# A re-planned adaLN transformer block: second-norm scalings with a GpSimd alternative, a 6/2 split of the modulation weight load, and a new order plan

## The chip, the cores and the metric

The kernel runs on one core of a Trainium2 chip. A core has TensorE (PE in the profile, with its weight loads shown as PEld), VectorE (DVE), ScalarE (ACT), GpSimd (POOL), and SyncE (SP), which here only issues transfers. The metric is the device time of one execution in microseconds.

## The reference

One transformer block on 2048 tokens of width 1024. Six modulation vectors come from a small conditioning vector; attention has 32 query heads of width 32 and one shared key and value head; the feed-forward part has a hidden width of 3584.

```
mod = silu(c) @ w_mod                      # 6 vectors of 1024: sa, ca, ga, sb, cb, gb
h = layernorm(x) * (1 + ca) + sa
q, k, v = h @ wq, h @ wk, h @ wv           # 32 heads of 32 for q, one head of 32 for k and v
x = x + ga * (softmax(q k^T / sqrt(32)) v @ wo)
h = layernorm(x) * (1 + cb) + sb
x = x + gb * ((silu(h @ w1) * (h @ w3)) @ w2)
```

## The kernel before, in words

**Blocks and stages.** The tokens are cut into 8 blocks of 256 (`n`), the heads into 8 groups of four (`f`), the keys into 8 pairs of 128 (`j`). One score step is eight matmuls (`s_exp`): four heads side by side on 32 rows each, two key tiles. There are 8 x 8 x 8 = 512 of them, and each is followed by two ACT exponentials of 128x1024 (tile U<-S). DVE adds pairs of the exponentials (tag `pair`, tile PS<-U) and sums those (tag `av`, PS<-PS), so that PE needs few matmuls for the softmax sums (PB<-PS,ONES); PE also multiplies with V (PB<-U,V). After the eighth head group of a block, `wo` projects, adds to x, and takes the second norm; `slab` (14 per block) does the gate and up products with tanh on ACT and two DVE multiplications; `quarter` (4 per block) does the product with w2. The feed-forward part of block n is laid beside the attention of block n+1, and that of the last block stands alone at the end.

**Second norm.** `wo(n)` makes the normalised rows in XN. For blocks 1 to 6, SP transposes them by two DMA transposes into tile QT (through `h2t`), and then eight VectorE instructions, one per 128 channels, multiply by 1+cb and add sb in place (QT<-QT,MODC, 128x256 bf16; 48 in all). The gate and up matmuls of a block read these eight pieces two at a time and in order. Blocks 0 and 7 go through TensorE transposes and are scaled while being read from PSUM.

**Start of the program.** SP issues the loads in one fixed list: x rows, parts of w_mod, parts of wq. `wm_dma(fld, h)` loads one modulation field in two parts of its eight 128-row chunks, cut by `WSPL`; field 1 is the scale ca, field 0 the shift sa. `mod_cols(fld)` is one group of matmuls per part. The scale goes into the key, value and first query weights (`scale0`), the shift into the biases of k and q (`k_bias`), which the first score needs. The list is: x 0-1, x 2-3, field 1 part 0, x 4-5, field 1 part 1, x 6-7, wq first part, x 8-11, field 0 part 0, field 0 part 1, wq second part, x 12-15.

**What sets the order.** Nothing is ordered by hand after that. The program first records all operations as a graph (`Graph.op`: engine, estimated duration, what is read and written, a due value `vt`, and `alts`, other engines that could do it). `Placer` then walks through a model of the time and decides at build time in which order, and for operations with `alts` on which engine, each is issued. Among operations that could start within a slack of the earliest, it takes the one with the least due value; score matmuls have the least of all. The estimated costs are the durations given to `op`, a price for PE when it changes between score matmuls (mode S), the attention products (mode A) and full matmuls (mode F) (`SWITCH`), and latencies between engines. For POOL it lengthens an operation that starts while a `pair` or `av` addition is on DVE. The steering numbers are in `PLAN`: one entry for each 16 score steps, with two slacks for starts, two rules for changes of mode, and additions to the due values by tag and engine (for example `"slab/pe": -12`). The result is one fixed instruction list per engine; on the chip, each engine works through its own list in order and waits on semaphores.

In `Placer.choose`, an entry is read like this:

```
late, pes, sl, one, hold, off = self.plan[min((self.step + self.SPAN - 1) // self.SPAN, len(self.plan) - 1)]
slack = pes if e == "pe" else sl
```

In profile rows nearly all instructions have line 22, since a helper there plays the recorded calls, so groups are told by tile names.

Of the kernel before, what the change touches and what calls it, by code (L numbers as in the profile page):

```python
# [6 lines left out]
ALU = mybir.AluOpType  # L7
# [35 lines left out]
class Graph:  # L43
# [63 lines left out]
    def alias(self, new, old):  # L107
# [5 lines left out]


PLAN = [
    (0.0, 0.12, 0.2, 1, 0.7,
     {"wo/pe": -19, "mc/pe": 25, "slab/dve": -28, "ln/dve": -40, "k/pe": 5, "mod/pe": 114, "mc/dve": 1}),
    (0.0, 0.12, 0.1, 1, 1.3, {"mc/pe": 27, "q/dve": -2, "ln/pe": 6, "ln/act": 32, "v/pe": 15, "mod/pe": 18}),
    (0.0, 0.12, 0.1, 1, 0.9,
     {"mc/pe": 27, "slab/act": -5, "q/dve": -2, "ln/pe": 6, "ln/act": 32, "v/pe": 15, "mod/pe": 18}),  # L120
    (0.0, 0.12, 0.1, 1, 0.9,
     {"q/pe": -119, "mc/pe": 27, "slab/act": -5, "q/dve": -2, "ln/pe": 6, "ln/act": 32, "v/pe": 15, "mod/pe": 18,
      "kb/pe": -44, "mc/dve": -51}),
    (0.0, 0.16, 0.2, 1, 2.6,
     {"slab/pe": -74, "q/pe": 2, "av/dve": 20, "slab/dve": 32, "slab/act": -7, "q/dve": -2, "mc/dve": 6}),
    (0.0, 0.16, 0.2, 1, 1.6,
     {"slab/pe": -74, "q/pe": 2, "av/dve": 20, "slab/dve": 32, "slab/act": -7, "q/dve": -2, "mc/dve": 6}),
    (0.0, 0.16, 0.2, 1, 1.3,
     {"slab/pe": -74, "q/pe": 2, "av/dve": 20, "slab/dve": 32, "slab/act": -7, "q/dve": -2, "mc/dve": 6}),
    (0.0, 0.13, 0.2, 1, 1.3,  # L130
     {"slab/pe": -74, "q/pe": 2, "av/dve": 20, "slab/dve": 32, "slab/act": -7, "wo/dve": 106, "q/dve": -2,
      "mc/dve": 6}),
    (0.0, 0.13, 0.2, 1, 1.3,
     {"slab/pe": -74, "q/pe": 2, "pair/dve": 22, "av/dve": 20, "slab/dve": 49, "slab/act": -7, "wo/dve": 106,
      "q/dve": -2, "mc/dve": 6}),
    (0.0, 0.11, 0.0, 1, 2.4, {"wo/pe": 4, "slab/pe": 107, "quarter/pe": -2, "q/pe": -26, "an/dve": 4, "q/dve": -119}),
    (0.0, 0.11, 0.02, 1, 2.6,
     {"wo/pe": 4, "slab/pe": 107, "quarter/pe": -2, "q/pe": -26, "an/dve": 4, "q/dve": -119}),
    (0.0, 0.11, 0.02, 1, 2.6,
     {"wo/pe": 4, "slab/pe": 107, "quarter/pe": -2, "q/pe": -26, "an/dve": 4, "q/dve": -119}),  # L140
    (0.0, 0.11, 0.2, 1, 2.6,
     {"wo/pe": 135, "quarter/pe": 20, "mc/pe": -8, "pair/dve": 119, "av/dve": -14, "an/dve": 72,
      "quarter/dve": -26, "wo/dve": 65, "q/dve": -66}),
    (0.0, 0.11, 0.2, 1, 1.4, {"wo/pe": -20, "slab/pe": 107, "q/pe": -26, "an/dve": 54, "q/dve": -119}),
    (0.0, 0.11, 0.02, 1, 3.1,
     {"wo/pe": -20, "q/pe": -26, "mc/pe": -3, "av/dve": 8, "an/dve": 54, "slab/dve": 29, "q/dve": -119}),
    (0.0, 0.11, 0.05, 0, 2.3,
     {"av/pe": -15, "q/pe": -9, "mc/pe": 109, "pair/dve": -1, "an/dve": 4, "slab/act": 15, "q/dve": 7,
      "mc/dve": 6}),
    (0.0, 0.11, 0.2, 1, 2.4,  # L150
     {"wo/pe": 17, "quarter/pe": -15, "mc/pe": -8, "pair/dve": -39, "av/dve": 1, "an/dve": 72,
      "quarter/dve": -26, "wo/dve": 65, "q/dve": -72}),
    (0.0, 0.12, 0.2, 1, 1.3, {"slab/pe": -12, "av/dve": 57}),
    (0.0, 0.11, 0.2, 1, 2.9,
     {"av/pe": -12, "wo/pe": -19, "slab/pe": -9, "quarter/pe": -39, "pair/dve": -2, "an/dve": -117,
      "quarter/dve": -16, "q/dve": -105}),
    (0.0, 0.11, 0.2, 1, 1.9,
     {"av/pe": -12, "wo/pe": -19, "slab/pe": -9, "quarter/pe": -39, "pair/dve": -2, "an/dve": -117,
      "quarter/dve": -16, "q/dve": -105}),
    (0.0, 0.11, 0.2, 1, 1.9,  # L160
     {"av/pe": -12, "wo/pe": -19, "slab/pe": -9, "quarter/pe": -39, "pair/dve": -2, "an/dve": -117,
      "quarter/dve": -16, "q/dve": -105}),
    (0.0, 0.11, 0.2, 0, 0.7,
     {"av/pe": -12, "wo/pe": -19, "slab/pe": -9, "quarter/pe": -39, "pair/dve": -2, "an/dve": -143,
      "quarter/dve": -16, "q/dve": -105}),
    (0.0, 0.11, 0.05, 1, 3.1,
     {"wo/pe": -17, "mc/pe": -8, "av/dve": 1, "an/dve": 47, "slab/act": 11, "quarter/dve": -26, "wo/dve": 86}),
    (0.0, 0.11, 0.05, 1, 3.1,
     {"wo/pe": -17, "mc/pe": -8, "av/dve": 1, "an/dve": 47, "slab/act": 11, "quarter/dve": -26, "wo/dve": 86}),
    (0.0, 0.11, 0.05, 1, 3.1,  # L170
     {"wo/pe": -17, "mc/pe": -8, "av/dve": 1, "an/dve": 47, "slab/act": 11, "quarter/dve": -26, "wo/dve": 86}),
    (0.0, 0.14, 0.2, 0, 0.1, {"slab/pe": -12, "pair/dve": -20, "av/dve": -18, "slab/dve": -24}),
    (0.0, 0.11, 0.05, 0, 3.3,
     {"wo/pe": -17, "mc/pe": -8, "pair/dve": 43, "av/dve": 14, "slab/act": 9, "quarter/dve": -26}),
    (0.0, 0.11, 0.05, 0, 3.3,
     {"wo/pe": -17, "mc/pe": -8, "pair/dve": 43, "av/dve": 14, "slab/act": 9, "quarter/dve": -26}),
    (0.0, 0.11, 0.2, 1, 1.4,
     {"av/pe": -15, "quarter/pe": -3, "q/pe": -9, "mc/pe": 33, "pair/dve": -16, "av/dve": -5, "an/dve": 18,
      "quarter/dve": -37, "q/dve": 7, "mc/dve": 6}),
    (0.0, 0.11, 0.2, 1, 1.4,  # L180
     {"quarter/pe": -3, "q/pe": -9, "mc/pe": 33, "av/dve": -5, "an/dve": 18, "quarter/dve": 74, "q/dve": 7,
      "mc/dve": 6}),
    (0.0, 0.11, 0.0, 1, 1.4,
     {"quarter/pe": -3, "q/pe": -9, "mc/pe": 33, "av/dve": -5, "an/dve": 18, "quarter/dve": 74, "q/dve": 7,
      "mc/dve": 6}),
    (0.0, 0.11, 0.05, 0, 4.1,
     {"wo/pe": -17, "slab/pe": -70, "mc/pe": -8, "pair/dve": 43, "av/dve": 14, "slab/dve": 97, "slab/act": 9,
      "quarter/dve": -26}),
    (0.0, 0.11, 0.2, 0, 3.3,
     {"slab/pe": -13, "quarter/pe": 27, "mc/pe": 61, "slab/dve": -16, "quarter/dve": 6, "wo/dve": 2}),  # L190
]


# [257 lines left out]
def build(nc, x_in, wq_in, wk_in, wv_in, wo_in, w1_in, w3_in, w2_in, c_in, wmod_in, out, S, D, F):  # L451
    G = Graph(nc)
    op = G.op
    NC = D // P
# [43 lines left out]
    MODC = sb("MODC", [P, 4, NC], F32)  # L498
# [87 lines left out]
        dma("sp", dst, x2[tt0 * P:(tt0 + cnt) * P, :].rearrange("(t p) d -> p t d", p=P), ("XL", tt0),  # L586
            cnt * P * D * 2, writes=keys, vt=vt, bw=FAST)

    WSPL = (0, 4, NC)

    def wm_dma(fld, h, vt):
        c0, c1 = WSPL[h:h + 2]
        dma("sp", WM0[:, c0:c1, fld * D:(fld + 1) * D], pc(wmod_in)[:, c0:c1, fld * D:(fld + 1) * D],
            ("WM0", fld, h), (c1 - c0) << 18, writes=[("WM0", fld, h)], vt=vt, bw=FAST)

    def wq_dma(f0, f1, key, vt):
# [18 lines left out]
       writes=["C1"], vt=-1990)  # L615
    op("dve", lambda: [lambda e: e.tensor_scalar(SCC[:, 2, :], SCC[:, 1, :], 0.5, 0.5, ALU.mult, ALU.add)], 0.17,
       reads=["C1"], writes=["C2"], vt=-1990)
    op("dve", lambda: [lambda e: e.tensor_tensor(SCC[:, 3, :], SCC[:, 2, :], SCC[:, 0, :], ALU.mult)], 0.17,
       reads=["C0", "C2"], writes=["C3"], vt=-1990)
    op("dve", lambda: [lambda e: e.tensor_copy(WKR[:, 0], WKV[:, 0].unsqueeze(2).broadcast_to([P, NC, 4, 32]))], 0.45,  # L620
       reads=[("WKV", 0)], writes=["WKR0"], vt=-1600)
# [297 lines left out]
    def h2t(n):  # L919
        return H20 if n == 0 else QT[:, n - 1, :, :]  # L920

    def h2k(n):
        return [("H20", cc) for cc in range(NC)] if n == 0 else [("QT", n - 1, cc) for cc in range(NC)]

    def xk(n, t, qs=range(4)):
        return [("X", n % NX, t, q) for q in qs]

    def wo(n, vt):
        G.tag = "wo"
        for t in range(2):  # L930
            for h in range(2):
                s = Sess()
                for q in range(4):
# [3 lines left out]
                       reads=[(k, *i) for f in range(2 * q, 2 * q + 2) for k, i in (("QT", (n, f)), ("WOG", (f,)))],  # L937
                       writes=[("wo", n, t, h)], vt=vt, mode="F", sess=s, post=0.145)
                xs = X1[:, n % NX, t, h * 512:(h + 1) * 512]
                k = xk(n, t, (2 * h, 2 * h + 1))  # L940
                op("dve", lambda b, xs=xs: [lambda e: e.tensor_tensor(xs, xs, BANK[b], ALU.add)], 0.605,
                   reads=[("wo", n, t, h)] + k, writes=k, vt=vt, sess=s)
            ln_stats(X1[:, n % NX, t, :], 2 * n + t, xk(n, t), vt)
            ln_norm(X1[:, n % NX, t, :], 2 * n + t, xk(n, t), t, vt)
        if 0 < n < NB - 1:
            for t in range(2):
                o = op("sp", lambda t=t: [lambda e: e.dma_start_transpose(h2t(n)[:, :, t * P:(t + 1) * P], XN[t])], 1.2,
                       reads=[("XN", t)], writes=[("h2r", n, t)] + h2k(n), vt=vt - 100, waw=(t == 0), dma=("HT2", t),
                       nbytes=1 << 18)
                o.bw = 200e3  # L950
            for cc in range(NC):
                op("dve", lambda cc=cc: [lambda e: e.tensor_scalar(
                    h2t(n)[:, cc, :], h2t(n)[:, cc, :], MODC[:, 3, cc:cc + 1], MODC[:, 2, cc:cc + 1], ALU.mult, ALU.add)],
                   0.17, reads=[("h2r", n, 0), ("h2r", n, 1), ("MODC", 3, cc // 4), ("MODC", 2, cc // 4)],
                   writes=[h2k(n)[cc]], vt=vt)
            return
        for hh in range(2):
            s = Sess()
# [3 lines left out]
               writes=[("h2", n, hh)], vt=vt, mode="F", sess=s, post=0.145)  # L962
            for k in range(4):
                cc = 4 * hh + k
# [3 lines left out]
                   reads=[("h2", n, hh), ("MODC", 3, hh), ("MODC", 2, hh)], writes=[h2k(n)[cc]], vt=vt, sess=s)  # L968
# [136 lines left out]
    for cc in range(NC):  # L1105
        op("dve", lambda cc=cc: [lambda e: e.tensor_scalar(WQ[:, cc, :], WQ[:, cc, :], MODC[:, 1, cc:cc + 1], None,
                                                           ALU.mult)], 0.43,
           reads=["WQ0", "WQ1", ("MODC", 1)] + [("QBI", f) for f in range(NC)], writes=["WQ0", "WQ1"], vt=-1100,
# [16 lines left out]
    for f in range(NC):  # L1125
        op("dve", lambda f=f: [lambda e: e.tensor_tensor(WO[:, f, :], WO[:, f, :], GAR[:], ALU.mult)], 0.605,
           reads=[("WO", f // 4), ("XN", 0)], writes=[("WOG", f)], vt=20)
# [77 lines left out]
```

## Time and profile before

| what | value |
|---|---|
| median of 3 runs | 1142.18 us (1142.15 to 1142.33) |
| profiled execution | 1142.53 us |
| its span, first to last instruction | 1140.7 us |
| PE, ACT, DVE, POOL busy | 1115.7, 1024.3, 953.9, 38.3 us |
| granted TensorE clock | 1.000 |
| first exponential starts | 30.97 us |
| span 41 to 200 us: PE, ACT busy of 159 | 151.81, 158.37 us |
| span 200 to 1045 us: PE, ACT busy of 845 | 836.15, 829.14 us |
| span 1045 to 1141 us: PE, ACT busy of 96 | 92.76, 8.37 us |

A row of the groups gives busy time, the mean length of one instruction in ns, and the idle time of the engine just before it with what ended that idle time. Lengths of neighbours overlap in the pipeline, so busy time divided by the count is what one of them takes from its engine.

### The profile page before, as it was taken

Reading aid. Unit: us, or ns where it says so; the run is one execution under the profiler, and the core shown is the slowest. Engines: PE = TensorE matmul, PEld = TensorE weight load, DVE = VectorE, ACT = ScalarE, POOL = GpSimd, SP = SyncE. Lnnn points to the kernel's source line nnn. Section 1 sums busy time; section 2 is a strip of 40 time slices with the busy share of each in tenths; the row PEclk is TensorE's granted clock in tenths of the full one; section 3 lists DMA queues with packets and bytes.
Section 4 is the critical chain, followed back from the end, with each engine's and each line's share of the span. In section 5 each row is a group of like instructions: output and inputs, shape, how many; then the busy total and the mean of one; then the engine's idle time right before and its main releaser. Section 6 shows DMA issues by size and latency. Waiting matters only on the chain.

```text
span 1140.7 us, 34695 instructions
## 1 busy us (share of the span) xinstructions
PE 1115.7 (98%) x15538; PEld 756.8 (66%) x15568; DVE 953.9 (84%) x1557; ACT 1024.3 (90%) x1161; POOL 38.3 (3%) x83
## 2 busy tenths in 40 slices
PE   8999999999999999999999999999999999999998
PEld 7644556666577756776567656776577656776887
DVE  7888899998888888888979799888978988888442
ACT  5999999999999999999999999999999999996110
POOL 4100000000000000000000010000100000000000
PEclk9999999999999999999999999999999999999999
DMA  9500379665596668665696659675686658667793
GB/s 345 179 2 1 113 222 245 181 187 155 132 264 194 172 163 221 191 196 154 145 253 196 173 143 236 192 204 131 156 249 192 174 140 231 194 188 202 222 291 118
DMA packets 374291, 209.45 MB, mean 184 GB/s; under 512 B 17536, under 2 KB 365952, under 8 KB 374144
## 3 DMA queue, kind: packets, MB, share of 16 engines
q1 hardware_dynamic: 373712, 207.11, 65.2%
q8 instruction: 122, 2.00, 0.8%
q14 instruction: 25, 0.20, 0.1%
q10 hardware_dynamic: 432, 0.13, 0.0%
HBM read 199.89 MB, written 4.19 MB: 179 GB/s over the span
## 4 chain that ended last, share of the span: by engine, by line
ACT 48%; PE 41%; DVE 8%; DMA 2%; issue 1%; SPq 0%; POOL 0%; DVEq 0%
ACT U L22 44%; PE PB L22 29%; PE S L22 12%; DVE PS L22 4%; ACT HT L22 4%; DVE QT L22 1%; DMA W<-in_A_wq_dram 1%; DVE HT L22 1%; DVE RB L22 1%; DVE X L22 0%; DMA QT<-XNB 0%; SPq L22 0%; DVE ST L22 0%; DVE XNB L22 0%; DVE RC L22 0%
## 5 line engine op out<-in xcount | busy, mean ns | idle before, releaser
L22 ACT ACTIVATE U<-S 128x1024 bf16<-128x1024 f32 x1024 | 962.8, 1105 | 15.7 <-PE S L22 7.7
L22 DVE TENSOR_TENSOR PS<-U 128x2048 bf16<-128x2048 bf16 x256 | 309.1, 1213 | 21.3 <-ACT U L22 19.2
L22 DVE TENSOR_TENSOR PS<-PS 128x1024 bf16<-128x1024 bf16 x368 | 248.9, 685 | 4.0
L22 PE MATMUL PB<-QT,W 128*128 128x256 bf16 x1856 | 230.6, 273 | 0.9 <-DVE RB L22 0.4
L22 PE MATMUL S<-QT,KT 32*128 32x256 bf16 x4096 | 203.4, 273 | 7.8 <-ACT U L22 5.5
L22 PEld LDWEIGHTS PB<-QT,W 128*128 128x128 bf16 x1856 | 169.9, 98 | 49.3 <-issue 26.8
L22 PE MATMUL PB<-W2S,HT 128*128 128x256 bf16 x1512 | 189.8, 273 | 0.0
L22 PEld LDWEIGHTS PB<-W2S,HT 128*128 128x128 bf16 x1512 | 136.9, 98 | 43.8 <-issue 27.2
L22 PEld LDWEIGHTS S<-QT,KT 32*128 32x128 bf16 x4096 | 60.7, 92 | 134.8 <-ACT U L22 122.4
L22 PE MATMUL PB<-U,V 128*32 128x256 bf16 x4032 | 125.6, 273 | 1.6 <-DVE HT L22 1.0
L22 PE MATMUL PB<-QT,HT 128*128 128x256 bf16 x960 | 120.6, 273 | 0.6 <-DVE HT L22 0.3
L22 PEld LDWEIGHTS PB<-U,V 128*32 128x32 bf16 x4032 | 99.7, 96 | 23.4 <-issue 10.8
L22 ACT ACTIVATE HT<-PB 128x512 bf16<-128x512 f32 (+1 forms) x110 | 76.4, 696 | 32.7 <-PE PB L22 32.6
L22 PEld LDWEIGHTS PB<-QT,HT 128*128 128x128 bf16 x960 | 87.7, 98 | 25.8 <-issue 14.0
L22 PE MATMUL PB<-HT,W 128*128 128x256 bf16 (+1 forms) x561 | 98.5, 316 | 2.4 <-issue 1.6
L22 DVE SCALAR_TENSOR_TENSOR HT<-HT,PB 128x512 bf16<-128x512 bf16 x102 | 69.4, 681 | 31.8 <-ACT HT L22 30.9
L22 DVE TENSOR_TENSOR HT<-HT,PB 128x512 bf16<-128x512 bf16 x102 | 69.5, 682 | 15.0 <-PE PB L22 13.2
L22 PEld LDWEIGHTS PB<-HT,W 128*128 128x128 bf16 x576 | 50.2, 97 | 37.0 <-issue 13.9
L22 PE MATMUL PB<-WO,QT 128*128 128x512 bf16 x217 | 54.0, 380 | 1.8 <-issue 1.3
L22 DVE STREAM_TRANSPOSE RB<-PB 128x256 f32<-128x256 f32 x63 | 28.2, 447 | 29.6 <-PE PB L22 29.4
L22 POOL TENSOR_SCALAR RS<-MV 128x1 f32<-128x1 f32 x32 | 11.3, 354 | 1015.4 <-DVE MV L22 1010.4
L22 DVE COPY RB<-PB 128x256 f32<-128x256 f32 x63 | 26.4, 419 | 18.5 <-PE PB L22 18.5
(112 smaller groups left out, 648.9 us busy)
## 6 DMA issues: line engine op xcount, KB each, us to landing
W<-in_B_w_dram SPq DMA_DIRECT2D x150, 512.0 KB, 4.9
W2S<-in_B_w_dram SPq DMA_DIRECT2D x28, 1792.0 KB, 8.3
HT<-in_B_w_dram SPq DMA_DIRECT2D x74, 512.0 KB, 4.9
W2S<-in_w_mod_dram SPq DMA_DIRECT2D x8, 1024.0 KB, 6.8
X<-in_A_x_dram SPq DMA_DIRECT2D x8, 512.0 KB, 6.3
U<-in_w_mod_dram SPq DMA_DIRECT2D x4, 1024.0 KB, 11.4
out_dram<-X SPq DMA_DIRECT2D x7, 512.0 KB, 7.9
U<-in_B_w_dram SPq DMA_DIRECT2D x1, 3584.0 KB, 14.0
```

What stands on the lines that cost most here:

```text
L22: return getattr(e, call[0])(*call[1], **call[2])
```

## The change

Three things change.

The eight scalings per block are given an estimated cost of 0.258 in place of 0.17, and an alternative: the same instruction on POOL at an estimated 0.8. The planner chooses for each. The line `POOLH = True` switches the alternative on.

The cut of the modulation loads moves from 4+4 chunks to 6+2, for both fields (1.5 MB and 0.5 MB in place of 1 MB and 1 MB).

All entries of `PLAN` are replaced (the rest of the new list is left out below). The chooser and its rules stay the same.

```diff
 PLAN = [
-    (0.0, 0.12, 0.2, 1, 0.7,
-     {"wo/pe": -19, "mc/pe": 25, "slab/dve": -28, "ln/dve": -40, "k/pe": 5, "mod/pe": 114, "mc/dve": 1}),
-    (0.0, 0.12, 0.1, 1, 1.3, {"mc/pe": 27, "q/dve": -2, "ln/pe": 6, "ln/act": 32, "v/pe": 15, "mod/pe": 18}),
...
+    (0.0, 0.2, 0.2, 0, 1.3, {"mc/pe": -16, "pair/dve": -90, "av/dve": -32, "k/pe": -82, "k/dve": 48, "mod/pe": 53}),
+    (0.0, 0.16, 0.2, 1, 1.3, {"mc/pe": 77, "pair/dve": -90, "q/dve": -23, "k/pe": -82, "k/dve": 48, "mod/pe": 53}),
...
-    WSPL = (0, 4, NC)
+    WSPL = (0, 6, NC)
...
+    POOLH = True
...
             for cc in range(NC):
                 op("dve", lambda cc=cc: [lambda e: e.tensor_scalar(
                     h2t(n)[:, cc, :], h2t(n)[:, cc, :], MODC[:, 3, cc:cc + 1], MODC[:, 2, cc:cc + 1], ALU.mult, ALU.add)],
-                   0.17, reads=[("h2r", n, 0), ("h2r", n, 1), ("MODC", 3, cc // 4), ("MODC", 2, cc // 4)],
-                   writes=[h2k(n)[cc]], vt=vt)
+                   0.258, reads=[("h2r", n, 0), ("h2r", n, 1), ("MODC", 3, cc // 4), ("MODC", 2, cc // 4)],
+                   writes=[h2k(n)[cc]], vt=vt, alts=[("pool", lambda cc=cc: [lambda e: e.tensor_scalar(
+                       h2t(n)[:, cc, :], h2t(n)[:, cc, :], MODC[:, 3, cc:cc + 1], MODC[:, 2, cc:cc + 1], ALU.mult,
+                       ALU.add)], 0.8)] if POOLH else [])
             return
```

More of the change, by code (lines that the diff above doesn't have):

```diff
@@ L115 @@
 PLAN = [
-    (0.0, 0.12, 0.2, 1, 0.7,
-     {"wo/pe": -19, "mc/pe": 25, "slab/dve": -28, "ln/dve": -40, "k/pe": 5, "mod/pe": 114, "mc/dve": 1}),
-    (0.0, 0.12, 0.1, 1, 1.3, {"mc/pe": 27, "q/dve": -2, "ln/pe": 6, "ln/act": 32, "v/pe": 15, "mod/pe": 18}),
[L119 to L140, printed above, removed]
@@ L141 @@
-    (0.0, 0.11, 0.2, 1, 2.6,
[L142 to L190, printed above, removed]
+    (0.0, 0.2, 0.2, 0, 1.3, {"mc/pe": -16, "pair/dve": -90, "av/dve": -32, "k/pe": -82, "k/dve": 48, "mod/pe": 53}),
+    (0.0, 0.16, 0.2, 1, 1.3, {"mc/pe": 77, "pair/dve": -90, "q/dve": -23, "k/pe": -82, "k/dve": 48, "mod/pe": 53}),
@@ new lines @@
+    (0.0, 0.11, 0.2, 0, 2.2,
+     {"wo/pe": 106, "q/pe": -78, "mc/pe": 6, "q/dve": 38, "ln/pe": -118, "ln/dve": 4, "mod/pe": -24}),
+    (0.0, 0.12, 0.2, 0, 0.7, {"wo/pe": 106, "q/pe": -78, "q/dve": 38, "ln/pe": -118, "ln/dve": 4}),
+    (0.2, 0.13, 0.2, 1, 0.8, {"q/pe": 47, "mc/pe": 46, "ln/act": -12, "k/pe": 22}),
+    (0.0, 0.13, 0.2, 1, 1.7, {"q/pe": 47, "mc/pe": 46, "pair/dve": -11, "av/dve": 4, "ln/act": -12, "k/pe": 22}),
+    (0.0, 0.13, 0.2, 1, 1.2,
+     {"slab/pe": -29, "q/pe": 47, "mc/pe": 46, "pair/dve": -11, "av/dve": 4, "slab/act": -66, "ln/act": -12,
+      "k/pe": 22}),
@@ new lines @@
+    (0.0, 0.11, 0.02, 0, 1.7, {"av/dve": 29, "an/dve": 55, "slab/dve": 1}),
+    (0.0, 0.11, 0.2, 0, 1.7, {"an/dve": 55, "slab/dve": 1}),
+    (0.0, 0.11, 0.2, 1, 1.4, {"av/dve": -11, "an/dve": 55, "slab/dve": 1, "q/dve": 9}),
+    (0.0, 0.11, 0.1, 0, 2.4,
+     {"wo/pe": 14, "slab/pe": 12, "quarter/pe": 3, "q/pe": -6, "av/dve": 18, "an/dve": 69, "slab/act": -1,
+      "quarter/dve": -7}),
+    (0.0, 0.11, 0.02, 0, 2.9, {}),
+    (0.0, 0.11, 0.2, 0, 2.9, {"wo/pe": 46, "an/dve": 55, "slab/dve": -89, "q/dve": 67}),
@@ new lines @@
+    (0.0, 0.11, 0.2, 1, 1.3, {"wo/pe": -13, "pair/dve": 6, "an/dve": 55, "slab/dve": -89, "q/dve": 67}),
+    (0.0, 0.11, 0.1, 1, 2.7,
+     {"slab/pe": -132, "q/pe": 47, "mc/pe": 46, "pair/dve": -13, "av/dve": 23, "slab/dve": -39, "slab/act": -20,
+      "quarter/dve": -47, "ln/act": -12, "k/pe": 22}),
+    (0.0, 0.11, 0.1, 1, 2.3,
+     {"slab/pe": -132, "q/pe": 47, "mc/pe": 46, "pair/dve": -13, "av/dve": -84, "slab/act": -20,
+      "quarter/dve": -47, "ln/act": -12, "k/pe": 22}),
+    (0.0, 0.11, 0.2, 1, 4.1,
+     {"wo/pe": 138, "slab/pe": -132, "quarter/pe": 13, "q/pe": 47, "mc/pe": 46, "pair/dve": -13, "av/dve": -83,
+      "slab/dve": -39, "slab/act": -20, "quarter/dve": -47, "ln/act": -12, "k/pe": 22}),
@@ new lines @@
+    (0.0, 0.11, 0.2, 1, 1.3,
+     {"slab/pe": -124, "q/pe": 47, "mc/pe": 46, "pair/dve": -24, "av/dve": -89, "an/dve": -26, "slab/dve": -39,
+      "slab/act": -20, "ln/act": -12, "k/pe": 22}),
+    (0.0, 0.11, 0.05, 1, 3.7,
+     {"wo/pe": -5, "quarter/pe": 48, "pair/dve": -3, "av/dve": -2, "slab/act": -7, "wo/dve": 20}),
+    (0.0, 0.11, 0.05, 1, 3.7,
+     {"wo/pe": -5, "quarter/pe": 48, "pair/dve": -3, "av/dve": -2, "slab/act": -7, "wo/dve": 20}),
+    (0.0, 0.11, 0.2, 1, 2.6,
+     {"wo/pe": 112, "slab/pe": -124, "quarter/pe": 26, "q/pe": 20, "mc/pe": 46, "pair/dve": 13, "av/dve": -89,
+      "an/dve": -26, "slab/dve": -39, "slab/act": -20, "quarter/dve": 35, "wo/dve": -2, "ln/act": -12,
+      "k/pe": 22}),
@@ new lines @@
+    (0.0, 0.11, 0.2, 1, 1.3,
+     {"slab/pe": -124, "quarter/pe": 26, "q/pe": 52, "mc/pe": 46, "pair/dve": 13, "av/dve": -72, "an/dve": -26,
+      "slab/dve": -39, "slab/act": -20, "quarter/dve": 35, "wo/dve": -6, "ln/act": -12, "k/pe": 22}),
+    (0.0, 0.11, 0.05, 1, 2.6,
+     {"slab/pe": -124, "quarter/pe": 26, "q/pe": 20, "mc/pe": 46, "av/dve": -89, "slab/dve": -39,
+      "slab/act": -20, "quarter/dve": 35, "ln/act": -12, "k/pe": 22}),
+    (0.0, 0.11, 0.05, 1, 1.4,
+     {"slab/pe": -124, "quarter/pe": 26, "q/pe": 20, "mc/pe": 5, "av/dve": -89, "slab/act": -20,
+      "quarter/dve": 35, "ln/act": -12, "k/pe": 22}),
@@ new lines @@
+    (0.0, 0.11, 0.2, 0, 1.6, {"wo/pe": 74, "pair/dve": 40, "av/dve": -2, "an/dve": 55, "slab/dve": -102, "q/dve": 6}),
+    (0.0, 0.11, 0.2, 1, 1.4, {"wo/pe": -13, "pair/dve": 40, "av/dve": -2, "an/dve": 55, "slab/dve": -88}),
+    (0.0, 0.11, 0.05, 1, 1.9,
+     {"slab/pe": -124, "quarter/pe": -21, "q/pe": 20, "mc/pe": 46, "pair/dve": 43, "av/dve": -89,
+      "slab/dve": -39, "slab/act": -20, "quarter/dve": 35, "ln/act": -12, "k/pe": 22}),
+    (0.0, 0.11, 0.05, 1, 1.9,
+     {"slab/pe": -124, "quarter/pe": -21, "q/pe": 20, "mc/pe": 46, "pair/dve": 43, "av/dve": -89,
+      "slab/act": -20, "quarter/dve": 35, "ln/act": -12, "k/pe": 22}),
@@ new lines @@
+    (0.0, 0.11, 0.2, 0, 3.4, {"wo/pe": 61, "q/pe": -20, "pair/dve": 3, "slab/dve": -23, "wo/dve": 33}),
+    (0.0, 0.11, 0.2, 1, 1.4, {"wo/pe": -5, "quarter/pe": 48, "pair/dve": -20, "av/dve": -27, "slab/act": -7}),
+    (0.0, 0.11, 0.05, 0, 2.1,
+     {"slab/pe": -124, "quarter/pe": -21, "q/pe": 20, "mc/pe": 46, "pair/dve": 43, "av/dve": -89,
+      "slab/dve": -39, "slab/act": -20, "quarter/dve": 35, "q/dve": -75, "ln/act": -12, "k/pe": 22}),
+    (0.0, 0.11, 0.05, 0, 4.0,
+     {"slab/pe": -124, "quarter/pe": -21, "q/pe": 20, "mc/pe": 46, "pair/dve": 43, "av/dve": -89,
+      "slab/act": -20, "quarter/dve": 35, "q/dve": -75, "ln/act": -12, "k/pe": 22}),
@@ L191 @@
+    (0.0, 0.11, 0.2, 0, 3.7,
+     {"wo/pe": -4, "slab/pe": -43, "q/pe": 20, "mc/pe": 46, "pair/dve": 43, "av/dve": 55, "slab/dve": -39,
+      "slab/act": -20, "quarter/dve": 35, "q/dve": -75, "ln/act": -12, "k/pe": 22}),
 ]
```

## The prediction

> **What bounds the kernel now.** First the page: which engine is full, and where.
>
> ```profile
> span 1140.7 us, 34695 instructions
> PE 1115.7 (98%) x15538; PEld 756.8 (66%) x15568; DVE 953.9 (84%) x1557; ACT 1024.3 (90%) x1161; POOL 38.3 (3%) x83
> ...
> PE   8999999999999999999999999999999999999998
> ...
> ACT  5999999999999999999999999999999999996110
> ```
>
> PE is full to the end. ACT is nearly as full until about 1045 us, and then PE works alone for 96 us on the last block. So a microsecond counts where PE waits, changes mode, or is held back by ACT; POOL is idle. Next, busy time by stretch: from 41 to 200 us ACT has 158.37 of 159 us, so there ACT sets the pace. From 200 to 1045 us PE lacks 8.9 us of 845 and ACT 15.9, so PE sets it, with ACT close behind.
>
> A full PE need not be an efficient one, so next the order of the matmuls, from the timeline (start, length, group):
>
> ```profile
> 300.55 1.93 PE L22 MATMUL PB<-U,V 128*32 128x256 bf16 x64
> 302.41 0.40 PE L22 MATMUL S<-QT,KT 32*128 32x256 bf16 x8
> 302.74 1.48 PE L22 MATMUL PB<-W2S,HT 128*128 128x256 bf16 x12
> 304.16 0.40 PE L22 MATMUL S<-QT,KT 32*128 32x256 bf16 x8
> 304.49 0.40 PE L22 MATMUL PB<-PS,ONES 128*32 128x256 bf16 x8
> 304.82 1.05 PE L22 MATMUL PB<-W2S,HT 128*128 128x256 bf16 x8
> 305.80 0.40 PE L22 MATMUL S<-QT,KT 32*128 32x256 bf16 x8
> ```
>
> Twelve full matmuls take 1.48 us and eight 1.05, so one takes 0.1075. Twelve are 1.29, but the next score group starts 1.42 after them: entering costs 0.13. Eight small matmuls are 0.21 (63 steps of the first row in 1.66 us), but the group after a score group starts 0.33 later: leaving costs 0.12. A change of mode is therefore about 0.12 us. Going through the whole trace in order of start I count 512 score runs and 1115 changes; with exactly one run of one kind between every two score groups there would be 1022. The third to sixth rows show an extra one: a sum group and full matmuls in the same gap. So 93 changes, 11.2 us, are the most that a better order can save there.
>
> The chain of waits then shows the place that the edit touches:
>
> ```profile
> 308.20 2.05 DVE QT L22 x8
> ...
> 429.76 4.77 DMA QT<-XNB
> 434.56 2.14 DVE QT L22 x8
> ...
> 944.61 2.05 DVE QT L22 x8
> ```
>
> All six sets of scalings stand on the chain (those left out start at 560.71, 689.68 and 817.50): at each block's start, PE soon runs into feed-forward matmuls that need them.
>
> **Part 1, the planned cost of the scalings (0.17 to 0.258).** Eight take 2.13 us on DVE, 0.267 each (12.8 us over 48 in the groups), against 1.36 planned. PE's list was laid for the shorter time, so PE must wait. Fourth block, from the timeline:
>
> ```profile
> 689.60 2.13 DVE L22 TENSOR_SCALAR QT<-QT,MODC 128x256 bf16<-128x256 bf16 x8
> 690.30 1.88 PE L22 MATMUL PB<-QT,HT 128*128 128x256 bf16 x8
> ```
>
> Eight matmuls take 1.88 in place of 1.05: 0.83 us lost. The same for the other five (blocks from 308, 434, 560, 817, 944 us): 0.35, 0.59, 0, 0, 0.10. The sum is 1.87 us. A plan with the right cost can put other matmuls there, if any are left. I take **-1.9 us**, bounds 0 (nothing left to put there) and -1.9. DVE's own time does not change by this.
>
> **Part 2, the POOL alternative.** The planner gives an operation to the engine that can start it first. With DVE at 0.258 and POOL at 0.8, about six of eight go to DVE and two to POOL. The nearest POOL rows (min/median/max ns):
>
> ```profile
> L22 POOL TENSOR_SCALAR RS<-MV x32: 222/224/1081, 6.3 to 1059.1; 128x1 f32<-128x1 f32 x32
> L22 POOL TENSOR_TENSOR RS<-RS,NH x32: 568/568/1448, 6.7 to 1059.4; 128x1 f32<-128x1 f32 x32
> L22 POOL TENSOR_SCALAR PS<-W,MODC x2: 963/986/1010, 17.9 to 18.9; 128x256 bf16<-128x256 bf16 x2
> ```
>
> The third row is the very shape, at the start, while DVE ran the same kind: 0.986, not 0.8. Two in a row are 1.97 us, against 2.13 for eight on DVE: 0.16 sooner per block, 1.0 us over six, since DVE's six end at 1.60. Best end: -0.53 x 6 = -3.2 us, if POOL keeps pace. The first two rows give the bad end: the same one-column instruction takes 0.22 alone and 1.08 at most, 0.57 and 1.45; I read the difference, 0.86, as POOL held while DVE adds (the 1.08 us one at 678.44 lies beside an addition PS<-U of 1.17 us that DVE starts at 678.27). DVE is free for those additions again 1.60 us after the start, when POOL's second piece still has 0.4 to go. Twelve pieces held for 0.86 would be +10.3 us. PE takes its list in order, so a late piece stops all matmuls behind it, scores too, and ACT after its two buffers. I take two or three such delays (2.3 us) less the 1.0: **+1.3 us**, bounds -3.2 and +10.3. That the planner's model of POOL covers a delay when the operation starts, but not an addition that starts later, is why I do not take the better end. The DVE time given free, 12 x 0.267 = 3.2 us, is hidden: DVE is at 84%.
>
> The Trainium skill speaks against this part: "GPSIMD Engine Reference", section 1, says POOL's interfaces to the on-chip memory are shared with VectorE and contend with instructions that have two inputs there. The stretched rows above agree. Its section 4.1 says that one-input work on POOL runs at about line rate; the 0.986 against 0.267 us here disagrees, and the row decides.
>
> **Part 3, the 6+2 split.** The two shift loads land 12.4 and 13.9 us after issue at 10.70 and 11.96 us (least and greatest of that tile in the window from 8 to 31 us), so at 23.1 and 25.8; four chunks arrive in 2.7 us, 0.68 each. The matmuls of four chunks (32) take 2.08 us, 0.52 a chunk. Before:
>
> ```profile
> 25.88 2.02 PEld L22 LDWEIGHTS PB<-SCC,U 128*128 128x128 bf16 x32
> ```
>
> They start as the second part lands and end at 27.9. After: six chunks land at 23.1 + 1.36 = 24.5, end at 27.6, and two more end at 28.6, for the last byte still lands at 25.8. That is 0.7 us later; the shift then goes into the key and query biases, the first score, and the exponentials at 30.97, and from 41 us ACT has no gap to make it up. For the scale (field 1) the last part is shorter: 1.04 us sooner from 13.28 on, but its next user, the first query weight, lands at 17.7 and hides that. x rows 4 and 5 land 1.4 us later, behind a larger first part; their norm is needed only for later keys. I take **+0.6 us**, bounds -1.0 (the shorter last part wins after all, because PE does other work in between) and +0.7.
>
> **Part 4, the new plan.** Every entry changes, so everything from the first instruction may move. What it can reach: 11.2 us of extra changes and PE's idle time from 41 to 1045 us, 7.2 + 8.9 us; together 27 us. PE is already at 98% and ACT has only 15.9 us of room from 200 to 1045, so half, 14, is the best end. On the other side, the plan is laid on estimated costs, and part 1 shows one place where an estimate cost 1.9 us; two such places give +4. I take a sixth of the 27, **-4.5 us**, near the small end because little is left. It comes as fewer changes of mode and a shorter leftover of older blocks when the exponentials end.
>
> **The sum.** -1.9 + 1.3 + 0.6 - 4.5 = -4.5 us. From the profiled execution (1142.53, span 1140.7 and 1.8 around it) that is 1138.0. The median is 0.35 lower, well inside the range, and I leave 1138.0.
>
> **Rivals.**
> 1. *POOL holds PE* (slower, 0.20). Decides where a POOL piece outlasts the six on DVE and an addition starts meanwhile. At half of the twelve, +5.2 us, with parts 1 and 4 worth nothing and the split at +0.6: 1142.5 + 5.8 = 1148; with a third of the order's gain, 1146. For: the stretched rows, and all six sets on the chain. Against: the reading order lets PE start on the first pieces, and the planner may leave pieces with DVE.
> 2. *Nothing left to win, or the parts do not bite* (within 0.2%, 0.23). PE is at 98%, POOL gets few pieces, the new order trades changes against waits: parts 1 and 3 alone give 1142.5 - 1.3 = 1141.
> 3. *The order is worth more* (under 1133.5, 0.04): at half of the 27 us, 1142.5 - 14 = 1129.
>
> **How the numbers follow.** The forecast, and gains around it beyond 0.2%, have 0.53. About 0.2% (2.3 us) is what a measurement can tell from no change here, so 1139.9 to 1144.5 is "same". Faster: 0.53 + 0.04 = 0.57; same 0.23; slower 0.20. The range, 1133.5 to 1146, takes in the forecast's bounds, rival 2 and the milder half of rival 1, and leaves out the deep gain and POOL at its worst.
>
> **What would show it.** Right: fewer than 1115 changes of mode, PE's idle time under 25 us, the exponentials' end before 1045, DVE rows QT<-QT,MODC near 36, and POOL rows of that tile near 1 us. Wrong: POOL rows of 1.5 us and more with PE groups PB<-QT stretched beside them; a first exponential before 30.97 us (part 3); as many changes of mode as before, or more idle time of PE between 200 and 1045 us (part 4).

## The result, and the profile after

The changed kernel takes 1134.9 us (median of 4, 1134.71 to 1135.67) against 1142.16 (median of 4, 1141.78 to 1142.33): ratio 0.9938, 95% interval 0.9922 to 0.9954, 7.3 us faster. The forecast was 1138.0. The profiled execution took 1134.8 us with a span of 1133.0, so 7.7 us of span are to be explained.

First the page, with the two slice rows:

```profile
span 1133.0 us, 34735 instructions
PE 1116.9 (99%) x15568; PEld 760.1 (67%) x15568; DVE 955.7 (84%) x1546; ACT 1020.6 (90%) x1159; POOL 53.5 (5%) x96
...
PE   8999999999999999999999999999999999999998
...
ACT  5999999999999999999999999999999999996110
```

The shares of PE, ACT and DVE are within 1% of those before; POOL's busy time goes from 38.3 to 53.5 us. Something else on the page moves, the chain that ended last, by engine, here before and after:

```profile
ACT 48%; PE 41%; DVE 8%; DMA 2%; issue 1%; SPq 0%; POOL 0%; DVEq 0%
```

```profile
PE 70%; ACT 25%; DVE 2%; DMA 1%; POOL 0%; issue 0%; SPq 0%; POOLq 0%
```

How the chain divides between PE and ACT says little (a run below with the same order has ACT at 61% and PE at 35%). DVE's part is steadier: 8% before, 2% after, and 7% again in the run below that gives POOL's pieces back to DVE.

One trap: PE's count is 15568 here and 15538 before, while the weight loads are 15568 both times. The 30 missing records are matmuls of 512 columns (about 6.4 us of streaming), so of the 25.0 us of PE's idle time before, up to 6.4 were no idle time. The fall from 25.0 to 16.1 must not be read as a gain of 8.9.

A safer measure: the 512 score groups come in the same sequence in every version, so the time at which the n-th starts (counted from 0, read from the trace) says where time is won.

| start of score (us) | 0 | 8 | 128 | 192 | 256 | 320 | 384 | 448 | 511 | after it to the end |
|---|---|---|---|---|---|---|---|---|---|---|
| before | 30.49 | 50.44 | 278.50 | 406.78 | 533.82 | 664.06 | 791.91 | 917.29 | 1041.95 | 98.77 |
| after | 31.09 | 50.07 | 278.94 | 405.09 | 531.46 | 657.61 | 783.75 | 909.90 | 1034.23 | 98.78 |

Up to score 128 the new kernel is 0.4 us behind; from there to 511 it wins 8.2; the stretch after the last score is the same. From score 128 on, a block of 64 scores took between 125.4 and 130.2 us before; now every one takes 126.1 to 126.4. The groups of PE behind the pieces are the same in all six blocks (six full matmuls, four on the pieces, a score, fourteen).

I then filled in the missing records and compared the gap between the starts of every two neighbouring matmuls with the usual gap for their kinds. What is beyond the usual falls from 30.2 to 23.8 us, and the changes of mode from 1115 to 1105 (1.2 us at 0.12 each): 7.6 of the 7.7 us. The usual gap is a choice, so the two sums depend on it; their difference says that it is mostly waits, hardly modes.

The start of a feed-forward block shows it. Timeline of the new kernel, with POOL:

```profile
305.04 1.22 DVE L22 TENSOR_TENSOR PS<-U 128x2048 bf16<-128x2048 bf16 x1
305.06 2.31 POOL L22 TENSOR_SCALAR QT<-QT,MODC 128x256 bf16<-128x256 bf16 x2 [3.93 <-DMA QT<-XNB]
306.18 1.78 DVE L22 TENSOR_SCALAR QT<-QT,MODC 128x256 bf16<-128x256 bf16 x6
...
306.65 0.83 PE L22 MATMUL PB<-W2S,HT 128*128 128x256 bf16 x6
307.32 0.60 PE L22 MATMUL PB<-QT,HT 128*128 128x256 bf16 x4
...
308.33 1.70 PE L22 MATMUL PB<-QT,HT 128*128 128x256 bf16 x14
```

The planner gave POOL two of eight pieces in each of the six blocks. PE's first matmuls on them run at full rate (14 in 1.70 us; the fourth block before had 8 in 1.88). On the chain of waits, only one of the six sets is left among the longest pieces:

```profile
428.08 4.36 DMA QT<-XNB
432.46 1.86 DVE QT L22 x6
```

The POOL rows after the change (min/median/max ns):

```profile
L22 POOL TENSOR_SCALAR QT<-QT,MODC x12: 595/608/1722, 305.1 to 937.7; 128x256 bf16<-128x256 bf16 x12
...
L22 POOL TENSOR_SCALAR PS<-W,MODC x3: 918/964/999, 16.9 to 18.8; 128x256 bf16<-128x256 bf16 x3
```

Seven of the twelve take 0.6 us, not 0.986. In five of the six blocks the first one takes 1.72: it starts under one of DVE's additions PS<-U (305.04 to 306.26 in the timeline above) and ends 0.5 us after it.

### The profile page after: what moved, and what is told of

It is laid out like the page before. It is cut to its first block, busy times and chain, and to the rows that moved or that the text cites. A ratio compares the mean times of both kernels' runs of the same rounds, so it can differ in the third digit from the quotient of the medians.

```text
span 1133.0 us, 34735 instructions
## 1 busy us (share of the span) xinstructions
PE 1116.9 (99%) x15568; PEld 760.1 (67%) x15568; DVE 955.7 (84%) x1546; ACT 1020.6 (90%) x1159; POOL 53.5 (5%) x96
## 4 chain that ended last, share of the span: by engine, by line
PE 70%; ACT 25%; DVE 2%; DMA 1%; POOL 0%; issue 0%; SPq 0%; POOLq 0%
PE PB L22 53%; ACT U L22 24%; PE S L22 17%; DMA W<-in_A_wq_dram 1%; DVE PS L22 1%; ACT HT L22 1%; DMA QT<-XNB 0%; DVE X L22 0%; SPq L22 0%; POOL PS L22 0%; DVE ST L22 0%; DVE QT L22 0%; DVE HT L22 0%; POOL RS L22 0%; DVE RB L22 0%
## 5 line engine op out<-in xcount | busy, mean ns | idle before, releaser
L22 PE MATMUL PB<-HT,W 128*128 128x256 bf16 (+1 forms) x576 | 101.8, 318 | 0.2
L22 DVE STREAM_TRANSPOSE RB<-PB 128x256 f32<-128x256 f32 x63 | 28.2, 448 | 38.5 <-PE PB L22 38.3
L22 PE MATMUL PB<-WO,QT 128*128 128x512 bf16 x232 | 57.3, 381 | 0.0
L22 PEld LDWEIGHTS PB<-WO,QT 128*128 128x128 bf16 x232 | 19.8, 97 | 25.0 <-issue 7.2
```

What stands on the lines that cost most here:

```text
L22: return getattr(e, call[0])(*call[1], **call[2])
```

## The experiments

Three theories. A: the new plan entries make the gain. B: POOL's share makes it. C: the right cost makes it. A change of cost or engine also changes every later choice of the planner, so two kinds of run are needed: with the order *worked out anew*, and with the order *kept*. In a kept-order run the planner is told the old numbers and only the issued instructions differ:

```diff
+        n.plan_eng = e                 # what the planner reckons with
+        if n.real is not None:
+            e, fn = n.real             # what is issued, at the same place of the order
+            n.eng = e
         self.emit(n, e, fn)
```

All medians, of five executions unless said, with the ratio to the kernel before on the same chip:

| run | us | ratio [95%] |
|---|---|---|
| all pieces on DVE, order kept | 1138.4 | 0.9962 [0.9949, 0.9974] |
| cut 4+4, order kept | 1136.6 | 0.9945 [0.9932, 0.9957] |
| changed kernel, old entries | 1163.38 | 1.0181 [1.0167, 1.0195] |
| before, new entries (4) | 1176.74 | 1.0298 [1.0284, 1.0313] |
| changed kernel again | 1135.06 | 0.9936 [0.9923, 0.9948] |
| four pieces on POOL, order kept | 1135.1 | 0.9929 [0.9915, 0.9942] |
| before, two pieces on POOL, order kept (11) | 1141.01 | 0.9985 [0.9976, 0.9993] |
| cut 4+4, head planned anew | 1136.6 | 0.9947 [0.9934, 0.9959] |
| filler on PE, order kept | 1135.16 | 0.9937 [0.9925, 0.995] |
| filler and four on POOL | 1134.4 | 0.9933 [0.9921, 0.9946] |
| before, right cost only (4) | 1174.52 | 1.028 [1.0266, 1.0294] |
| changed kernel without POOL, anew (4) | 1167.45 | 1.0223 [1.0207, 1.0239] |

### POOL's pieces back on DVE, order kept

```diff
-                   0.258, reads=..., alts=[("pool", ...)]
+                piece = op(... the same, planned with POOL ...)
+                piece.real = ("dve", the same instruction)
```

> The changed kernel with its order kept to the instruction, planned with POOL, but the 12 scalings that POOL does (pieces 1 and 5 of each of six blocks) are issued on DVE at the same place of the order. Theory A (the new order makes the gain, POOL's share is worth almost nothing): DVE has 84% and takes 12 x 0.267 = 3.2 us more spread over six blocks; PE's list has other matmuls there, so 1134.9 to 1136.5, scores fall behind by under 0.3 us a block. Theory B (POOL's share of the work on the chain of waits makes the gain): the eight take 2.13 us again in place of 1.86 for the six that DVE does, and PE waits for them: 2 to 4 us lost, 1137 to 1139.

Measured 1138.4, the price of theory B. Part of that is another start and another first block in this execution (1.3 us at score 128, see the clock below); the two executions whose mean clock stayed at 1.000 took 1136.68 and 1137.51. From score 128 on, it loses 0.35, 0.59, 0.35, 0.35, 0.36 and 0.33 us, in each of the six blocks and nowhere else: 2.3 us. (The second block is less sure than the others: its length moves by 0.2 us either way in runs that leave the pieces alone.) But in five of the six it does not go theory B's way. Waits of PE in the span from 200 to 1030 us (total, times, longest), first of the changed kernel, then of this one:

```profile
PE PB L22 <- DVE HT L22: 0.2, 1, 0.2
```

```profile
PE PB L22 <- DVE HT L22: 2.5, 6, 0.7
```

In these five PE does not wait for the scaled pieces (groups PB<-QT run at 14 in 1.70 here too); in the second it does, where four take 0.89 us in place of 0.60. In all six it waits later, for the multiplication that frees a bank of PSUM (the memory that matmuls write to), which comes late because DVE has been without a gap since the pieces:

```profile
307.72 1.87 DVE L22 TENSOR_SCALAR QT<-QT,MODC 128x256 bf16<-128x256 bf16 x7
...
314.18 1.06 PE L22 MATMUL PB<-U,V 128*32 128x256 bf16 x32 [0.34 <-DVE HT L22]
```

The first row leaves out the first of the eight pieces, which lies at the edge of this view. The second block:

```profile
435.10 0.89 PE L22 MATMUL PB<-QT,W 128*128 128x256 bf16 x4
435.59 0.11 PEld L22 LDWEIGHTS PB<-QT,W 128*128 128x128 bf16 x2 [0.40 <-DVE QT L22]
```

Two pieces are 0.54 us of DVE; 0.35 of it reaches PE. So most of what POOL's share is worth is DVE's time in a stretch where DVE is full, although it is 84% busy over the span.

### The mirror: the old order with two pieces on POOL

```diff
+                piece.real = ("pool", the same instruction) if cc in (1, 5) else None
```

> The kernel of before with its order kept to the instruction, but pieces 1 and 5 of each of the six blocks' scalings issued on POOL at the same place of the order. It is the mirror of the run with all pieces on DVE, which lost 0.35 us at each of six blocks (2.4 us). If POOL's share is worth that in any order: 1139.3 to 1140.5. If it pays only in an order that was laid for it (PE does not meet the pieces in three of the six blocks before): 1141 to 1142.2. If POOL's pieces come late (additions on DVE in between): above 1142.5.

1141.01 against 1142.62 on the same chip. By the scores, it wins 0.31, 0.25, 0.36, 0.27, 0.27 and 0.36 us in the six blocks, 1.8 in all, and nothing elsewhere. Here theory B's way is seen as well: where PE met the pieces in the old order, its groups on them get shorter, in the fourth block from 1.88 us to this:

```profile
689.47 1.61 PE L22 MATMUL PB<-QT,HT 128*128 128x256 bf16 x8
```

So POOL's share is worth 1.8 to 2.3 us in either order; the rest of the 8.2 us, about 6, is the order's (with the planned cost, which shaped it).

### Four pieces on POOL

```diff
+                piece.real = ("pool", the same instruction) if cc in (3, 7) else None   # beside 1 and 5
```

> The changed kernel with its order kept to the instruction, but pieces 1, 3, 5 and 7 of each six blocks' scalings on POOL (24 in all, not 12); pieces 3 and 7 leave DVE. The prediction's rival 1, a late piece stops PE: four pieces on POOL take at least 4 x 0.6 = 2.4 us, and one more addition may hold one by up to 1.1 us (the POOL rows after the change go from 0.595 to 1.722), so the last piece comes 2.4 to 3.5 us after the start, 0.5 to 1.6 us later than DVE's six (1.86). PE reads the last piece with the eighth matmul: 3 to 9 us lost over six blocks, 1138 to 1144. If there is room on PE before it needs pieces 5 and 7: 1134.9 to 1136.

1135.1 beside 1135.06. No loss, so rival 1 of the prediction, a late piece that stops PE, falls for this order. The timeline of the fourth set shows why:

```profile
685.02 1.22 DVE L22 TENSOR_TENSOR PS<-U 128x2048 bf16<-128x2048 bf16 x1
685.03 3.39 POOL L22 TENSOR_SCALAR QT<-QT,MODC 128x256 bf16<-128x256 bf16 x4 [3.91 <-DMA QT<-XNB]
686.15 1.27 DVE L22 TENSOR_SCALAR QT<-QT,MODC 128x256 bf16<-128x256 bf16 x4
...
688.30 1.70 PE L22 MATMUL PB<-QT,HT 128*128 128x256 bf16 x14
```

POOL is held by an addition that keeps DVE itself from starting until 686.15; after that POOL goes at 0.6 a piece, and the last is done at 688.4, as PE reaches it. From score 128 on, this run wins 0.65 us on the changed kernel; it started 1.7 us late. About 0.06 us of it comes in each block, 0.4 in all; the rest comes in the second block, whose length moves without any change of the pieces too.

### The old list in the changed kernel, the new list in the old

```diff
-PLAN = [ ... new entries ]
+PLAN = [ ... entries of before ]      # and the other way round in the second run
```

> The changed kernel with the list of plan entries of before: measured cost, POOL alternative and 6+2 cut stay, the order is worked out anew from the old entries. Theory A (the new entries make the gain): 1140 to 1144, blocks of unequal length as before the change. Theory C (the right cost and the POOL alternative make it, the entries only follow): 1135 to 1138, and the stalls of PE at the scalings are gone.

> The kernel of before with the new list of plan entries alone: cost 0.17, no POOL alternative, 4+4 cut. Theory A: 1135 to 1138, PE meeting scalings that are late by 0.8 us a block (0.3 us lost in each of six blocks on average before). Theory C: 1140 or more, since the same entries with a wrong cost and without POOL give another order.

1163.38 and 1176.74. In the first run both theories miss; in the second, theory C's "1140 or more" holds, but without a size, and the loss is greater than the forecast of every part. With the old list the scores end where they did before the change (the last at 1040.95), but 118.6 us of work are left after it in place of 98.8. With the new list in the old kernel the scores themselves fall behind, at the last one 35 us behind the changed kernel and 27 behind the old.

### The right cost alone, and the new list without POOL

```diff
-                   0.17, reads=[("h2r", n, 0), ...            # in the kernel before
+                   0.258, reads=[("h2r", n, 0), ...
...
-    POOLH = True                                           # in the changed kernel
+    POOLH = False
```

> The kernel of before with the scalings planned at 0.258 and nothing else: old plan entries, no POOL, 4+4 cut. Part 1 of the prediction in its literal form: up to 1.9 us less, 1140.3 to 1142.2. Against it, from the two runs with mixed lists: a list fits only the graph and the costs it was searched for, and one changed cost moves every later choice: 1150 or more, with a longer stretch after the last exponential.

> The changed kernel with the POOL alternative switched off and the order worked out anew from the new list. The run with all pieces on DVE in the kept order lost 2.4 us of the gain. If the list carries over: 1137 to 1139. If a list fits only the costs and choices of engine it was searched for: 1145 or more.

1174.52 and 1167.45, as the second expectation had it each time. In the first, the starts of the scores follow the kernel before within 0.01 us of a constant offset up to score 142. There the first of the 48 operations with the new cost comes (308 us), and the order goes another way: the last score is 11 us later and 120.6 us of work are left. In the second, the last score is 23.5 us behind that of the changed kernel, and 105.7 us are left. Theory C, taken alone, falls, as theory A does. The cost, the choice of engine and the list make a gain together; the four mixtures of old and new cost 21 to 35 us. Why an order that does not fit leaves so much more work behind the last score was not followed up.

### The cut

```diff
+    CUT = (0, 4, NC)          # really loaded and multiplied; planned with (0, 6, NC)
```

> The changed kernel with its order kept to the instruction, planned with the 6+2 cut, but the modulation fields are really loaded and multiplied as 4+4 chunks. The prediction's part 3: the first score and the first exponential come 0.6 to 0.7 us sooner (30.5 and 31.0 us, as before the change), since the four chunks of the last part start at 25.8 and end at 27.9. If the delay passes through to the end (ACT has no gap from 41 us on), the total is 1134.2 to 1134.4. Rival: the shorter last part pays elsewhere, or ACT's first 10 us have room: 1134.8 to 1135.6.

The first score came at 32.69, 1.6 us later and not sooner. The profiled execution does not tell what the cut does: PE's clock fell, as the next section shows, and the same start (32.80) was seen with 6+2 in the run with four pieces. The times tell more: the two executions whose mean clock stayed at 1.000 took 1135.23 and 1135.76, and those of the changed kernel in the same condition 1134.63 to 1135.06 (the three of the repeat in the table). So no gain of the cut 4+4 is seen in this order. What the profiled execution shows is that a late start passes to the end: 1.6 us at score 0, 1.6 at 192, 1.8 at the last.

```diff
-    WSPL = (0, 6, NC)
+    WSPL = (0, 4, NC)         # planned so too
```

> The changed kernel with the modulation cut 4+4 and the order worked out anew from the same plan entries; the instruction lists of PE differ in the first block alone (the first 105 of 1238 rows), and are the same after that. Part 3 of the prediction: the first score 0.6 us sooner than with 6+2, which passes through to the end as the 1.6 us of the kept-order run did: 1134.2 to 1134.4, better than both kernels. Rival: the first block's new order loses it again (the list was not tuned to it): 1135 to 1137.

The first score came 0.88 us sooner (30.21), but at score 8 the run was 1.1 us behind and at 64 1.5 us, and it ended at 1136.6 against 1135.06. Its clock stayed at 1.000 in four of the five executions (1135.98 to 1136.69), so it is not the clock. So the first score is not what decides: in the first block, the order of keys, queries and norms around the scores does, and the list came with 6+2. What the cut alone is worth with a list of its own stays open.

### The clock in two places

> The changed kernel once more, as the yardstick for the runs beside it on the same chip: 1134.9 by its first measurement. A spread of 1 us between executions is expected from the start of the program alone (first score between 31.0 and 31.6 us).

1134.63 to 1136.89, more than the expected 1 us. The two slowest (1135.72 and 1136.89) have a mean granted clock of 0.998, the other three 1.000 and 1134.63 to 1135.06. The profiled one, 1135.72, is equal to the first measurement to 0.03 us up to score 64 and then 0.9 us late. Busy time and granted clock (the eighth column, after POOL) by stretch, of this execution and then of the first one:

```profile
173.00:178.00 5.00, 3.44 (x68) 1.82 (x60) 4.93 (x16) 5.00 (x6) 0.90 (x2) 1.00 1.14 301
178.00:184.00 6.00, 5.60 (x51) 3.29 (x52) 5.01 (x10) 5.24 (x7) 0.00 (x0) 0.72 1.19 291
```

```profile
173.00:178.00 5.00, 3.41 (x68) 1.81 (x60) 4.93 (x16) 5.00 (x6) 0.90 (x2) 1.00 1.16 306
178.00:184.00 6.00, 5.44 (x62) 3.79 (x63) 5.87 (x12) 6.00 (x8) 0.00 (x0) 1.00 1.19 291
```

In both, PE is busy for 3.4 of 5 us; afterwards the clock is 0.72 in one and 1.00 in the other, and ten matmuls take 2.31 us in place of 1.32. The other place is the wait for the first part of wq. In the run with four pieces POOL's scaling of it began at 17.83 us, in the first execution of the changed kernel at 16.91; PE stood 2.3 us in place of 1.1, and then:

```profile
20.73 1.05 PE L22 MATMUL S<-HT,PS 128*128 128x256 bf16 x8 [2.27 <-POOL PS L22]
...
22.00:24.00 2.00, 2.00 (x16) 1.50 (x15) 1.44 (x4) 1.86 (x2) 1.08 (x4) 0.53 1.05 381
24.00:26.00 2.00, 2.00 (x19) 1.82 (x18) 1.11 (x3) 0.62 (x1) 0.80 (x2) 0.62 1.06 375
```

The first row is of its timeline, the others are of its stretches. In the run with the cut 4+4 and the kept order PE stood 2.46 us there and the clock fell too; in the run with all pieces on DVE it stood 2.11 us and the clock stayed at 1.00.

The Trainium skill, "TensorE: Matmul & The Clock Gate", Part 1, says that PE runs at half its rate after an idle window of some 3.4 us, and that the windows run freely, so that the moment of the change varies. The half rate agrees with the traces (a stretch of 6 us at 0.72 is 3.4 us at one half), and so does one program that falls into it in some executions only; but here gaps of 2.3 and 2.5 us, and a stretch with 70% of work, were enough.

So the filler, on PE alone:

```diff
-        op("pe", lambda: [lambda e: e.matmul(... IDENT ...)],
+        op("pe", lambda m=9 if i < 2 else 1: [lambda e: e.matmul(... IDENT ...) for _ in range(m)],
...
-                IDENT[:]) for t in range(2) for k in range(4)], 0.47,
+                IDENT[:]) for _ in range(3 if n == 0 and hh == 1 else 1) for t in range(2) for k in range(4)], 0.47,
```

> The changed kernel with its order kept, and filler on PE alone in the two places where its clock fell in some executions: 18 idle matmuls on the identity where there were 2, before the first query product, and the second set of eight transposes of the first block's norm done three times, where PE waits for ACT. Nothing else moves. Theory: the spread of the changed kernel (1134.6 to 1136.9) comes from these two places, 1.7 us where the first score is at 32.8 in place of 31.1, and 0.9 us in the score steps 64 to 80. With the clock held: all five between 1134.4 and 1135.2, first score at 31.1, granted clock 1.000. Rival: filler comes late itself and holds the first query product, or the clock falls for another reason: 1135 to 1137, spread as before.

1134.87 to 1135.32: the spread goes from 2.3 to 0.45 us and the mean clock is 1.000 in all five executions, but the median is no better (1135.16). In the profiled one the first score comes at 31.61, 0.5 us late. The load of wq was late again there (POOL's scaling began at 17.73), and PE, done with the filler, waits for the scaling:

```profile
17.73 2.85 POOL L22 TENSOR_SCALAR PS<-W,MODC 128x256 bf16<-128x256 bf16 x3 [1.41 <-DMA W<-in_A_wq_dram]
17.98 2.13 PE L22 MATMUL S<-IDENT 128*128 128x256 bf16 x18
20.65 1.05 PE L22 MATMUL S<-HT,PS 128*128 128x256 bf16 x8 [0.54 <-POOL PS L22]
```

So a late load costs some 0.5 us of the start by itself (0.4 in the run with all pieces on DVE, where the scaling began at 17.57 and the clock held). The run with four pieces, with a load as late and the fallen clock, started at 32.80: the clock is the other 1.2. Only 0.26 of the 0.5 us is left at the last score.

> The filler of the run before, and pieces 1, 3, 5 and 7 on POOL as in the run with four. That run gained 0.65 us from score step 128 to the end, behind a first score that was 1.7 us late. With the clock held, 1134.9 less 0.65: 1133.8 to 1134.6, faster than both kernels. Rival: the 0.65 was an accident of that execution's shifted times: 1134.4 to 1135.2.

1134.4 (1134.27 to 1135.37, the slowest with a mean clock of 0.998), the lowest median of the study. Beside the run with the filler alone it wins 0.38 us from score 128 on, 0.06 or 0.07 in each of the six blocks; so that of the 0.65 us of the run with four pieces some 0.4 are POOL's, and the rest was, as the rival had it, an accident of shifted times. It beats the kernel before by 0.9933 [0.9921, 0.9946]; against the changed kernel (1134.9 and 1135.06) the 0.4 us are shown by the starts of the scores in two executions, not by the intervals.

## Why the prediction was right, and where it was wrong

The direction and the range held. The gain was 7.7 us of span where 4.5 were forecast. Parts 1 and 4 together, which no run separates, were forecast at -6.4 and come out at about -5.9 (the 8.2 us less POOL's 2.3); part 3 at +0.6, measured +0.4 at score 128. So nearly the whole miss is part 2, whose sign was wrong: +1.3 forecast, -2.3 measured. That parts 1 and 4 agree so well is in part luck, for the share of 27 us that part 4 took was a choice.

**Part 1, the planned cost (-1.9).** The stalls went as forecast: the matmuls on the pieces run at full rate, and in five of six blocks even with all pieces on DVE. (The prediction's 0.35 us for the first block is 0.25 by the rows of that timeline, 4 in 0.69 and 12 in 1.64 us against 0.60 and 1.48; the sum is then 1.8.) But they do not go by the cost alone. "A plan with the right cost can put other matmuls there" was argued as if the order stayed the same; with the right cost and the old list the kernel took 1174.5. What the term is worth apart from the list can't be told.

**Part 2, POOL (+1.3).** The sign was wrong: -1.8 in the old order, -2.3 in the new, inside the bounds (-3.2 to +10.3). Two steps failed. The price 0.986 came from the start of the program and is 0.6 here where no addition holds the piece. And "the DVE time given free, 12 x 0.267 = 3.2 us, is hidden: DVE is at 84%" was the decisive error: behind the pieces DVE runs without a gap for more than 6 us, and the two pieces' 0.54 us per block reach PE as 0.35. The share over the span hid it. The rival's mechanism, a piece held by an addition, is real (1.72 us, in five of the six blocks), but the addition that holds POOL keeps DVE from its own pieces as well, so nothing comes later by it. The Trainium skill's line-rate sentence still does not hold: 0.6 against 0.267.

**Part 3, the cut (+0.6).** The step itself came out as worked: the matmuls start as the first part lands and end at 28.5 (28.6 forecast), and the first score is 0.59 us later.

```profile
24.54 3.93 PEld L22 LDWEIGHTS PB<-SCC,U 128*128 128x128 bf16 x64 [0.22 <-issue]
```

"From 41 us ACT has no gap to make it up" is half right: at score 8 the new kernel was 0.37 us ahead, at 128 0.44 behind. The cut 4+4 with the new list, with a sooner first score, was slower. The term was worked out for the first score; the end of the first block is what counts, and it hangs on the order.

**Part 4, the new plan (-4.5).** Of another make. The order gives about 6 us (8.2 less POOL's 2.3, with a start that is 0.4 behind), part 1's share in it. It was to come "as fewer changes of mode", of which 93 were counted as extra; 10 went, 1.2 us. The rest is waits by the count above. The longest block, from score 256 to 320, went from 130.2 to 126.15 us, but not by waits alone: it held 1809 matmuls and now holds 1793. One thing that the order ended can be seen at ACT. The waits of its exponentials for matmuls into tile PB, from score 128 to the last before the change, were these (total, times, longest), 4.0 us of them in that block:

```profile
ACT U L22 <- PE PB L22: 6.7, 3, 2.7
```

After the change there is none in the same stretch; how much of the gain this is was not worked out. "A shorter leftover of older blocks when the exponentials end" did not come: 98.77 and 98.78 us. Everything was won before the last score.

What stays open: why POOL takes 0.96 us for a piece at the start and 0.6 later (the one multiplies alone, the other multiplies and adds, in place), and the cut with a list of its own.

## What to carry to other kernels

A list of steering numbers belongs to the costs, engines and sizes it came with: a single corrected cost under the old list made this kernel 32 us slower, so judge such parts with the order kept and the issued instruction exchanged. An engine's share of the span does not say whether its time is free; look at the stretch behind the edit, and at who waits there for what that engine does next. When the same units of work come in the same sequence in two versions, the table of their start times tells where the time went before any theory does.

## What the runs showed of the hardware

PE's granted clock fell to a half for 3.4 us after gaps of 2.3 and 2.5 us (it stayed at 1.00 after one of 2.1), and after a stretch without such a gap in which PE was 70% busy; the latter in one execution of a program and not in another with the same times up to there. The two places cost 1.2 and 0.9 us. The changed kernel's executions without such a fall lie within 0.43 us (1134.63 to 1135.06), all five within 2.3. A piece on POOL that starts under one of DVE's additions with two inputs ends 0.5 us after the addition (0.6 us becomes 1.72); the addition itself takes no longer for it (1.22 us).
